# Decode step of a two-layer model: reordering the hand-over between layers, with fixed buffer slots and finer weight loads

## The chip, the cores and the metric

The kernel runs on one core of one Trainium2 chip. The metric is the device time of one execution in microseconds (us), lower is better. Before the change it is 533.6 us (median over 16 runs; 531.6 to 535.9 in the fast ones). One of those runs, the profiled one that the prediction was made from, took 668 us. It is of the slow state and is used in no comparison of times. Ratios below are the mean time of one kernel's fast runs over that of the other's fast runs of the same rounds, so they are not quite the ratio of the medians that are quoted.

## The reference

One token goes twice through attention and a gated MLP, with the same weights and the same caches both times. Cut to what matters:

```python
W = 4096                               # last W positions of a 32768-long cache
def attn(x):                           # 32 heads of 192; x is 1 x 640
    q = x @ wq                         # 640 -> 32*192
    s = einsum("hd,hkd->hk", q, k_cache[:, -W:]) * 192**-0.5
    return (softmax(s) @ v_cache[:, -W:]) @ wo
def mlp(x):  return (sigmoid(x @ w_gate) * (x @ w_up)) @ w_down      # 640 -> 1536 -> 640
for _ in range(2):
    x = x + attn(layernorm(x))
    x = x + mlp(layernorm(x))
```

There is one query per head, so nearly all the work is reading K and V: 16 head pairs, 7.3 MB each with their slices of `wq` and `wo`.

## The kernel before

All heavy data go through seven slots in SBUF (the on-chip memory), each of one unit of 3552 KB, plus a region `mreg` for MLP weights. Unit `a(p)` holds wq and K of head pair p, unit `b(p)` holds V and wo. At the end of layer 0 the seven slots are not freed: a(12) and a and b of pairs 13, 14 and 15 stay for layer 1, which therefore starts with these four pairs. V(12) is loaded again into `mreg` once the MLP is through with it.

```python
ORDER = [list(range(NPAIR)), [13, 14, 15, 12] + list(range(12))]
seq += stream(0, ORDER[0], [0])            # a0 a1 b0 a2 b1 ... a15 b14 b15 (two halves)
seq += [("wg",), ("u1",), ("u2",), ("d1",), ("d2",), ("va",), ("vb",), ("vc",)]
tail = stream(1, ORDER[1][4:], [0])        # layer 1: a0 a1 b0 a2 b1 ...
...
elif k == "u2":                            # second part of w_up, over the gate weights
    if "gate0" not in ev_done: return False
    pg.dma(... mreg(0, 5 * FW), wu_d[:, 7 * FW:] ...)
elif k in ("va", "vb", "vc"):              # V(12), over the MLP weights
    if "down0" not in ev_done: return False
```

The loads are issued from one queue, strictly in the order of `seq`; each waits until the region it overwrites has been read. TensorE, VectorE and ScalarE follow this loop:

```python
for i, p in enumerate(ORDER[l]):
    Q(p, y)              # 15 small matmuls: q of the pair
    QK(p, y)             # 24 matmuls 128x512, four column tiles side by side; then slot a(p) is free
    ...
    soft(p)              # maximum over the scores, exp
    ET(p, i % 2)         # transposes exp(scores)
    if prev is not None:
        PV(*prev)        # 32 matmuls 128x384 and the wo product of the pair before; then slot b is free
    prev = (p, i % 2)
```

In the MLP of layer 0 the gate is one block, and what overwrites it waits for all of it:

```python
proj(0, range(FC), g_of, 0, [...])         # gate: 12 blocks of 5 matmuls
if not last:
    mark("gate0")
```

## Time and profile before

| | slow profiled run | fast run |
|---|---|---|
| time, us | 668.0 | 533.6 (median) |
| bytes read from HBM | 219.18 MB | the same |
| rate while the DMA engines are full | 430 GB/s | not known before the prediction |
| one head pair in steady state | 19.26 us | not known before the prediction |

The page of the slow run: the busy time of the engines, then the span in 40 equal slices of 16.7 us. Each digit is the busy share in tenths, and GB/s is what the DMA engines moved.

```profile
span 666.2 us, 8191 instructions
PE 468.7 (70%) x3716; PEld 208.8 (31%) x3716; DVE 98.3 (15%) x372; ACT 88.6 (13%) x171; POOL 0.2 (0%) x4
...
DMA  8999999999999999360288784899899998995000
GB/s 357 436 432 429 426 430 434 429 430 429 429 437 426 426 432 371 148 290 1 110 293 325 311 363 184 363 409 399 363 371 370 370 367 387 416 369 226 0 1 3
```

For 250 us the DMA engines are full at about 430 GB/s. Then the stream has a hole between the layers, and never fills up again, because TensorE is slower than the stream in this run. The timeline of the same run shows one pair (start, duration, engine, line, operation; L350 is QK, L395 is PV):

```profile
104.89 4.92 PE L350 MATMUL scores<-big,qs 128*32 128x512 bf16 x24 [0.35 <-DVE qs L338]
...
116.12 4.90 PE L395 MATMUL bank<-big,et_sb 128*2 128x384 bf16 x32
...
124.17 4.91 PE L350 MATMUL scores<-big,qs 128*32 128x512 bf16 x24 [0.35 <-DVE qs L338]
```

From QK to QK it takes 19.28 us, but the pair's two units need only 2 x 3552 KB / 430 GB/s = 16.9 us. A run of 534 us is not possible at 19.3 us per pair (32 pairs would be 617 us), so in a fast run TensorE must be faster and the stream must bound. The stream alone needs 219.7 MB / 430 GB/s = 511 us. The question for the prediction was where the other 23 us of a fast run go.

### The profile page before, as it was taken

What the parts mean: (1) busy time and instruction counts of PE and PEld (TensorE: products, weight loads), DVE (VectorE), ACT (ScalarE), POOL (GpSimd) and SP (SyncE); (2) the same over time, 40 slices, a digit from 0 to 9 for tenths busy, and PEclk for the clock granted to TensorE, in tenths of its full rate; (3) what the DMA queues carried; (4) which work ended last, traced back from release to release, by engine and by line L of the source; (5) the groups of instructions that cost most, each with busy time, mean ns of one, the idle gap of its engine ahead of it and who ended that gap; (6) DMA issues with size and microseconds to landing.
All of it is one profiled execution on the core that took longest, in us unless ns stands there. A gap on an engine that the chain in (4) does not pass through costs nothing. (4 is left out here: it accounts for less than half of the span.)

```text
span 666.2 us, 8191 instructions
## 1 busy us (share of the span) xinstructions
PE 468.7 (70%) x3716; PEld 208.8 (31%) x3716; DVE 98.3 (15%) x372; ACT 88.6 (13%) x171; POOL 0.2 (0%) x4
## 2 busy tenths in 40 slices
PE   2676776777667677766765777667667766766776
PEld 1233232233223223332542323323223332233235
DVE  1111111110111111011012110111111011111101
ACT  0111111111111110111101011111110111111110
POOL 0000000000000000000000000000000000000000
DMA  8999999999999999360288784899899998995000
GB/s 357 436 432 429 426 430 434 429 430 429 429 437 426 426 432 371 148 290 1 110 293 325 311 363 184 363 409 399 363 371 370 370 367 387 416 369 226 0 1 3
DMA packets 10555, 219.71 MB, mean 330 GB/s; under 512 B 1304, under 2 KB 1304, under 8 KB 2200
## 3 DMA queue, kind: packets, MB, share of 16 engines
q1 hardware_dynamic: 10520, 219.19, 78.9%
q8 instruction: 29, 0.48, 0.3%
q14 instruction: 6, 0.05, 0.0%
HBM read 219.18 MB, written 0.00 MB: 329 GB/s over the span
## 5 line engine op out<-in xcount | busy, mean ns | idle before, releaser
L350 PE MATMUL scores<-big,qs 128*32 128x512 bf16 x768 | 157.7, 1046 | 11.0 <-DVE qs L338 10.5
L395 PE MATMUL bank<-big,et_sb 128*2 128x384 bf16 x1024 | 157.2, 855 | 0.0
L361 PE MATMUL bank<-diag,sc 128*128 128x128 f32 x64 | 32.2, 585 | 57.5 <-ACT diag L360 57.5
L395 PEld LDWEIGHTS bank<-big,et_sb 128*2 128x2 bf16 x1024 | 40.8, 164 | 74.2 <-issue 73.7
L359 DVE TENSOR_REDUCE sc<-scores 128x1 f32<-128x1024 f32 x32 | 39.2, 1225 | 151.6 <-PE scores L350 151.6
L350 PEld LDWEIGHTS scores<-big,qs 128*32 128x32 bf16 x768 | 34.8, 163 | 80.9 <-issue 67.6
L372 PE MATMUL bank<-cst,e_sb 128*128 128x8 bf16 x256 | 14.3, 179 | 61.5 <-ACT e_sb L366 61.5
L361 PEld LDWEIGHTS bank<-diag,sc 128*128 128x128 f32 x64 | 22.7, 395 | 110.0 <-ACT diag L360 110.0
L399 ACT CAST o_sb<-bank 128x384 bf16<-128x384 f32 x64 | 30.7, 479 | 196.5 <-PE bank L395 196.5
L360 ACT ACTIVATE diag<-cst,sc 128x128 f32<-128x128 bf16 x32 | 12.8, 401 | 267.2 <-DVE sc L359 267.2
L366 ACT ACTIVATE e_sb<-scores,sc 128x1024 bf16<-128x1024 f32 x32 | 38.5, 1204 | 52.2 <-DVE sc L364 52.2
L335 PE MATMUL bank<-sh,big 128*128 128x1 bf16 x480 | 29.5, 190 | 9.4 <-DMA big<-in_ua_dram 9.1
L379 PE MATMUL bank<-sc 128*128 128x2 f32 x64 | 24.8, 458 | 14.5 <-DVE sc L377 14.5
L372 PEld LDWEIGHTS bank<-cst,e_sb 128*128 128x128 bf16 x256 | 11.4, 119 | 70.9 <-ACT e_sb L366 70.9
L408 DVE TENSOR_SCALAR sh<-bank,sc 128x3 bf16<-128x3 f32 x32 | 7.2, 225 | 175.1 <-PE bank L405 175.1
L335 PEld LDWEIGHTS bank<-sh,big 128*128 128x128 bf16 x480 | 28.5, 153 | 9.5 <-DMA big<-in_ua_dram 9.2
L415 PE MATMUL bank<-sh,big 128*128 128x1 bf16 x480 | 23.8, 179 | 10.3 <-DVE sh L408 10.3
L379 PEld LDWEIGHTS bank<-sc 128*128 128x128 f32 x64 | 22.1, 385 | 17.5 <-DVE sc L377 17.5
L405 PEld LDWEIGHTS bank<-cst,o_sb 128*128 128x128 bf16 x192 | 7.6, 105 | 61.7 <-ACT o_sb L399 61.7
L415 PEld LDWEIGHTS bank<-sh,big 128*128 128x128 bf16 x480 | 21.1, 125 | 12.9 <-DVE sh L408 12.5
L405 PE MATMUL bank<-cst,o_sb 128*128 128x1 bf16 x192 | 10.2, 168 | 19.0 <-ACT o_sb L399 19.0
L362 DVE TENSOR_REDUCE sc<-bank 128x2 f32<-128x128 f32 x32 | 9.3, 292 | 49.1 <-PE bank L361 49.1
(55 smaller groups left out, 109.8 us busy)
## 6 DMA issues: line engine op xcount, KB each, us to landing
big<-in_ua_dram SPq DMA_DIRECT2D x28, 3552.0 KB, 20.8
big<-in_ub_dram SPq DMA_DIRECT2D x26, 3552.0 KB, 27.2
big<-in_ub_dram SPq DMA_DIRECT2D x2, 2016.0 KB, 7.4
big<-in_wg_dram SPq DMA_DIRECT2D x2, 1920.0 KB, 14.9
big<-in_ub_dram SPq DMA_DIRECT2D x2, 1536.0 KB, 10.7
big<-in_ub_dram SPq DMA_DIRECT2D x2, 1152.0 KB, 6.2
big<-in_wu_dram SPq DMA_DIRECT2D x1, 1920.0 KB, 14.4
big<-in_wu_dram SPq DMA_DIRECT2D x1, 1120.0 KB, 16.9
```

What stands on the lines that cost most here:

```text
L335: ins = t.matmul(qe[:, i:i + 1], lhsT=slot(sa, c * 2 * DH + c0, P), rhs=xq[:, c:c + 1], start=(c == 0), stop=(c == DC - 1))
L350: ins = t.matmul(bank[b][32 * j:32 * j + 32, :], lhsT=qs[:, y, k, :], rhs=slot(sa, WQE + k * W + (4 * b + j) * 512, 512), start=(k == 0), ...
L359: pg.op("dve", lambda v: v.reduce_max(out=mx, in_=scores[:], axis=AX.X), wr=[res("mx")], ex=[rb[0], rb[1]])
L360: pg.op("act", lambda a: a.mul(out=diag[:], in_=ident, mul=mx), rd=[res("cst"), res("mx")], wr=[res("diag")])
L361: pg.op("pe", lambda t: t.matmul(dmx[:, 0:P], lhsT=ones_f, rhs=diag[:], start=True, stop=True), rd=[res("diag"), res("ones")], ex=[rb[2]])
L366: pg.op("act", lambda a: a.activation(out=e_sb[:], in_=scores[:], func=ACT.Exp, bias=nbias, scale=srs_c, accum_out=rowsum), rd=[res("nbias ...
L372: ins = t.matmul(qe[:, 0:2 * NB].rearrange("p (r x) -> p r x", r=2)[:, :, 4 * b:4 * b + 4], lhsT=e_sb[:, b * P:(b + 1) * P], rhs=sel, star ...
L379: pg.op("pe", lambda t: t.matmul(dmx[:, P:P + 2], lhsT=ones_f, rhs=rs2, start=True, stop=True), rd=[res("rs2"), res("ones")], ex=[rb[2]])
L395: ins = t.matmul(o8[h][32 * j:32 * j + 2, 0:2 * DH].rearrange("p (a d) -> p a d", a=2), lhsT=et_sb[:, z, h * NB + 2 * u:h * NB + 2 * u + 2 ...
L399: pg.op("act", lambda a, h=h: a.copy(out=o8_sb[:, :, h * DH:(h + 1) * DH], in_=o8[h][:, 0:2 * DH].rearrange("p (a d) -> p a d", a=2)), wr= ...
L405: ins = t.matmul(oT3[:, c:c + 1], lhsT=o8_sb[:, sg, c:2 * DH:3], rhs=mask2[:, sg:sg + 1], start=(sg == 0), stop=(sg == 1))
L415: ins = t.matmul(yT[:, j:j + 1], lhsT=wo[:, c * D + j * P:c * D + (j + 1) * P], rhs=oTb[:, c:c + 1], start=False, stop=(c == 2), skip_grou ...
```

## The change

The intent is to keep the DMA queue full across the change of layer. The change has six parts: (1) the gate is cut into 5 + 7 blocks, and the loads over it wait for their own part; (2) the last V half of each layer is loaded and used in two quarters; (3) a(0) of layer 1 is loaded in two pieces, the first asked for after a third of QK(13); (4) the four kept pairs run in a new order, with QK(14) ahead of softmax 13 and its scores in the two PSUM banks of PV; (5) slots are assigned by a fixed table, with four slots in rotation in layer 0; (6) inside QK the loop over the three parts of the head dimension is the outer one. Cut to its core:

```diff
-    seq += [("wg",), ("u1",), ("u2",), ("d1",), ("d2",), ("va",), ("vb",), ("vc",)]
+    seq += [("wg", 0), ("wg", 1), ("u1",), ("u2",), ("d1",), ("d2",), ("va",), ("vb",), ("vc",)]
+    seq += [("a0", 0), ("a0", 1), ("wo12",)] + tail[1:]
+    A_SLOT = [{p: p % 2 ...}, ...]          # fixed slots; layer 0 rotates through four
...
-            mark("gate0")
+            mark("gate0", proj(0, range(GH), g_of, 0, [rm["a"]]))          # GH = 5
+            mark("gate1", proj(0, range(GH, FC), g_of, 0, [rm["b"]]))
...
-                for b in range(2):
-                    for k in range(3):
+                for k in ks:
+                    for b in range(2):
...
-        for i, p in enumerate(ORDER[l]):  ...    # one softmax at a time, also in layer 1
+            Q(13, 0); ...
+            mark("a13_0", QK(13, 0, ks=(0,)));  mark("a13_1", QK(13, 0, ks=(1, 2)))
+            Q(14, 1); ...; mark("Q12", Q(12, 0))
+            QK(14, 1, 1)                         # scores into the banks of PV
+            soft(0, scale_pm); expo(); Q(15, 1); ET(0)
+            soft(1); expo(1); QK(15, 1); PV(13, 0); ET(1)
+            soft(); expo(); PV(14, 1); QK(12, 0); ET(0)
+            soft(); expo(); PV(15, 0); Q(0, 0); ET(1); QK(0, 0); PV(12, 1); ...
```

No bytes are saved: both kernels read 219.18 MB.

More of the change, by code (lines that the diff above doesn't have):

```diff
@@ L1 @@
-from collections import deque
 from contextlib import ExitStack
@@ L155, in decode_kernel @@
     scores = ctx.enter_context(nc.psum_tensor("scores", [P, 1024], FP32))
-    bank = [scores[:, 0:512], scores[:, 512:1024]] + [ctx.enter_context(nc.psum_tensor(f"bank{i}", [P, 512], FP32)) for i in range(2, 8)]
+    bank = [scores[:, 0:512], scores[:, 512:1024]] + [ctx.enter_context(nc.psum_tensor(f"bank{i}", [P, 512], FP32)) for i in (2, 3)]
+    o8_ps = ctx.enter_context(nc.psum_tensor("o8", [P, 1024], FP32))
+    bank += [o8_ps[:, 0:512], o8_ps[:, 512:1024]] + [ctx.enter_context(nc.psum_tensor(f"bank{i}", [P, 512], FP32)) for i in (6, 7)]
     dmx, qe, o8, oT3, yT = bank[2], bank[3], bank[4:6], bank[6], bank[7]
@@ L167, in decode_kernel @@
     rslot = [res(f"slot{i}") for i in range(NSLOT)]
-    rm = {n: res("m_" + n) for n in ("a", "ax", "b", "c", "d")}
-    MOFF = {"a": (0, 3072), "b": (3072, 7680), "c": (7680, ME)}
+    rm = {n: res("m_" + n) for n in "abc"}
+    MOFF = {"a": (0, 5 * FW), "b": (5 * FW, 12 * FW), "c": (12 * FW, ME)}
     def slot(s, o, n):
@@ L180, in q_dma @@
         return lambda e: e.dma_start(out=o, in_=i)
-    RET = [("a", NPAIR - 4)] + [(k, p) for p in range(NPAIR - 3, NPAIR) for k in "ab"]
-    ORDER = [list(range(NPAIR)), [13, 14, 15, 12] + list(range(12))]
-    seq = []
-    def stream(l, ps, first):
-        out_ = [("a", l, p) for p in first]
-        q = deque(ps)
-        for p in ps[len(first):] if first else ps:
-            out_.append(("a", l, p))
-            out_.append(("b", l, q.popleft()))
-        last = list(q)
-        for p in last[:-1]:
-            out_.append(("b", l, p))
-        return out_ + [("b1", l, last[-1]), ("b0", l, last[-1])]
@@ L196, in decode_kernel @@
-    seq += stream(0, ORDER[0], [0])
-    seq += [("wg",), ("u1",), ("u2",), ("d1",), ("d2",), ("va",), ("vb",), ("vc",)]
-    tail = stream(1, ORDER[1][4:], [0])
-    seq += tail[:1] + [("wo12",)] + tail[1:]
+    A_SLOT = [{p: p % 2 for p in range(NPAIR)}, {p: 3 if p % 2 == 0 else 2 for p in range(NPAIR)}]
+    B_SLOT = [{p: 2 + p % 2 for p in range(NPAIR)}, {p: 5 if p % 2 else 0 for p in range(NPAIR)}]
+    A_SLOT[0].update({14: 4, 15: 6})
+    B_SLOT[0].update({14: 5, 15: 2})
+    A_SLOT[1].update({0: 1, 1: 4, **{p: A_SLOT[0][p] for p in (12, 13, 14, 15)}})
@@ new lines, in decode_kernel @@
+    B_SLOT[1].update({0: 6, **{p: B_SLOT[0][p] for p in (13, 14, 15)}})
+    KEPT = {(k, p) for p in (13, 14, 15) for k in "ab"} | {("a", 12)}
+    units = [("a", 0)] + [u for p in range(1, 12) for u in (("a", p), ("b", p - 1))] + [("b", 11), ("u", 0), ("d", 0)]
+    for i, (k, p) in enumerate(units):
+        s = (1, 0, 4, 6, 3, 5, 2)[(i if i == 0 else i + 1) % 7]
+        if k == "u":
+            U_SLOT = s
+        elif k == "d":
+            D_SLOT = s
+        else:
+            (A_SLOT if k == "a" else B_SLOT)[1][p] = s
@@ new lines, in decode_kernel, with stream @@
+    NHALF = NB * DH // 2
+    def stream(l, ps):
+        q = list(ps)
+        out_ = []
+        for i, p in enumerate(q):
+            out_.append(("a", l, p))
+            if i:
+                out_.append(("b", l, q[i - 1]))
+        return out_ + [("b1", l, q[-1]), ("b0", l, q[-1], 0), ("b0", l, q[-1], 1)]
+    seq = stream(0, range(NPAIR))
+    seq += [("wg", 0), ("wg", 1), ("u1",), ("u2",), ("d1",), ("d2",), ("va",), ("vb",), ("vc",)]
+    tail = stream(1, range(12))
+    assert tail[0] == ("a", 1, 0)
@@ L200, in decode_kernel, with wdp, take @@
+    seq += [("a0", 0), ("a0", 1), ("wo12",)] + tail[1:]
     seq += [("fg",), ("fu",), ("fd", 0), ("fd", 1), ("fd", 2)]
     seq_pos = [0]
-    free = deque(range(NSLOT))
-    where = {}
+    busy = set()
     ev_done = {}
-    fin = {}
-    wo12 = {}
-    halves = {}
-    pg_last = {}
-    def wdp(c0, c1, src=None):
-        return wd_d[:, c0 * D:c1 * D]
+    halves = {(0, NPAIR - 1), (1, 11)}
+    A0CUT = WQE + W
+    GH = 5
+    def wdp(c0, c1):
+        return wd_d[:, c0 * D:c1 * D]
+    def take(s):
+        if s in busy:
+            return False
+        busy.add(s)
+        return True
@@ L213, in try_load @@
     def try_load(it):
         k = it[0]
-        if k == "b0":
-            s = where[("b", it[2])]
-            pg.dma(q_dma(slot(s, 0, NB * DH), ub[it[2]][:, 0:NB * DH]), "bh", wr=[res("bh")], extra=list(pg_last["deps"].items()))
+        if k in ("a", "b"):
+            s = (A_SLOT if k == "a" else B_SLOT)[it[1]][it[2]]
+            if not take(s):
+                return False
+            pg.dma(q_dma(slot(s, 0, UNIT), (ua if k == "a" else ub)[it[2]]), f"s{s}", wr=[rslot[s]])
         elif k == "b1":
-            if not free:
-                return False
-            s = free.popleft()
-            where[("b", it[2])] = s
-            halves[(it[1], it[2])] = True
+            s = B_SLOT[it[1]][it[2]]
+            if not take(s):
+                return False
@@ L224, in try_load @@
             n = len(pg.ops["dma"])
             pg.dma(q_dma(slot(s, NB * DH, UNIT - NB * DH), ub[it[2]][:, NB * DH:]), f"s{s}", wr=[rslot[s]])
-            pg_last["deps"] = pg.ops["dma"][n]["deps"]
-        elif k in "ab":
-            if not free:
-                return False
-            s = free.popleft()
-            where[(k, it[2])] = s
-            pg.dma(q_dma(slot(s, 0, UNIT), (ua if k == "a" else ub)[it[2]]), f"s{s}", wr=[rslot[s]])
+            ev_done["b1"] = list(pg.ops["dma"][n]["deps"].items())
+        elif k == "b0":
+            s = B_SLOT[it[1]][it[2]]
+            o = it[3] * NHALF
+            pg.dma(q_dma(slot(s, o, NHALF), ub[it[2]][:, o:o + NHALF]), f"bh{it[3]}", wr=[res(f"bh{it[3]}")], extra=ev_done["b1"])
+        elif k == "a0":
+            if f"a13_{it[1]}" not in ev_done:
+                return False
+            s = A_SLOT[1][0]
+            o0, o1 = ((0, A0CUT), (A0CUT, UNIT))[it[1]]
+            pg.dma(q_dma(slot(s, o0, o1 - o0), ua[0][:, o0:o1]), f"a0{it[1]}", wr=[res(f"a0{it[1]}")] + ([rslot[s]] if it[1] else []),
+                   extra=[ev_done[f"a13_{it[1]}"]])
@@ L233, in try_load @@
         elif k == "wg":
-            pg.dma(q_dma(mreg(0, 12 * FW), wg_d), "wg", wr=[rm["a"], rm["ax"], rm["b"]])
+            f0, f1 = ((0, GH), (GH, FC))[it[1]]
+            pg.dma(q_dma(mreg(f0 * FW, (f1 - f0) * FW), wg_d[:, f0 * FW:f1 * FW]), f"wg{it[1]}", wr=[[rm["a"]], [rm["b"]]][it[1]])
         elif k == "u1":
-            pg.dma(q_dma(mreg(12 * FW, 7 * FW), wu_d[:, 0:7 * FW]), "u1", wr=[rm["c"], rm["d"]])
+            pg.dma(q_dma(mreg(12 * FW, 7 * FW), wu_d[:, 0:7 * FW]), "u1", wr=[rm["c"]])
@@ L239, in try_load @@
                 return False
-            pg.dma(q_dma(mreg(0, 5 * FW), wu_d[:, 7 * FW:]), "u2", wr=[rm["a"], rm["ax"]])
+            pg.dma(q_dma(mreg(0, 5 * FW), wu_d[:, 7 * FW:]), "u2", wr=[rm["a"]])
         elif k == "d1":
-            pg.dma(q_dma(mreg(5 * FW, 7 * FW), wdp(0, 7)), "d1", wr=[rm["b"]])
+            if "gate1" not in ev_done:
+                return False
+            pg.dma(q_dma(mreg(5 * FW, 7 * FW), wdp(0, 7)), "d1", wr=[rm["b"]], extra=[ev_done["gate0"]])
         elif k == "d2":
@@ L250, in try_load @@
             o0, o1 = MOFF[k[1]]
-            pg.dma(q_dma(mreg(o0, o1 - o0), ub[12][:, o0:o1]), k, wr={"a": [rm["a"]], "b": [rm["ax"], rm["b"]], "c": [rm["c"], rm["d"]]}[k[1]])
+            pg.dma(q_dma(mreg(o0, o1 - o0), ub[12][:, o0:o1]), k, wr=[rm[k[1]]])
         elif k == "wo12":
@@ L254, in try_load @@
                 return False
-            s = where[("a", 12)]
-            wo12["ap"] = slot(s, 0, WOE)
-            pg.dma(q_dma(wo12["ap"], ub[12][:, VE:UNIT]), "wo12", wr=[res("wo12")], extra=[ev_done["Q12"]])
+            pg.dma(q_dma(slot(A_SLOT[1][12], 0, WOE), ub[12][:, VE:UNIT]), "wo12", wr=[res("wo12")], extra=[ev_done["Q12"]])
         elif k == "fg":
-            pg.dma(q_dma(mreg(0, 12 * FW), wg_d), "wg", wr=[rm["a"], rm["ax"], rm["b"], rm["c"], rm["d"]])
+            pg.dma(q_dma(mreg(0, 12 * FW), wg_d), "fg", wr=[rm["a"], rm["b"], rm["c"]])
         elif k == "fu":
-            if not free:
+            if not take(U_SLOT):
                 return False
-            fin["u"] = s = free.popleft()
-            pg.dma(q_dma(slot(s, 0, 12 * FW), wu_d), f"s{s}", wr=[rslot[s]])
-        else:
-            if it[1] == 0:
-                if not free:
-                    return False
-                fin["d"] = free.popleft()
-            s = fin["d"]
+            pg.dma(q_dma(slot(U_SLOT, 0, 12 * FW), wu_d), f"s{U_SLOT}", wr=[rslot[U_SLOT]])
+        else:
+            if it[1] == 0 and not take(D_SLOT):
+                return False
             c0, c1 = WFIN[it[1]]
-            pg.dma(q_dma(slot(s, c0 * D, (c1 - c0) * D), wdp(c0, c1)), f"wf{it[1]}", wr=[rslot[s]] if it[1] == 0 else [])
+            pg.dma(q_dma(slot(D_SLOT, c0 * D, (c1 - c0) * D), wdp(c0, c1)), f"wf{it[1]}", wr=[rslot[D_SLOT]] if it[1] == 0 else [])
         return True
@@ L283, in release @@
     def release(s):
-        free.append(s)
+        busy.discard(s)
         prefetch()
@@ L327, in attention @@
         pg.op("dve", lambda v: v.memset(yT[:, 0:DC], 0.0), ex=[rb[7]])
+        S = [(scores, bank[0], bank[1], rb[0], rb[1]), (o8_ps, bank[4], bank[5], rb[4], rb[5])]
         def Q(p, y):
-            sa = where[("a", p)]
+            sa = A_SLOT[l][p]
             def f(t):
@@ L336, in f, with QK, soft @@
                 return ins
-            ev = pg.op("pe", f, rd=[res("xq"), rslot[sa]], ex=[rb[3]])
+            ev = pg.op("pe", f, rd=[res("xq"), rslot[sa]] + ([res("a00")] if l == 1 and p == 0 else []), ex=[rb[3]])
             pg.op("dve", lambda v: v.tensor_tensor(out=qs[:, y], in0=qe[:, 0:3].unsqueeze(2).to_broadcast([P, 3, 32]), in1=mask3, op=ALU.mult),
                   rd=[res("cst")], wr=[res(f"qs{y}")], ex=[rb[3]])
-            if l == 1 and p == 12:
-                mark("Q12", ev)
-        def QK(p, y):
-            sa = where[("a", p)]
+            return ev
+        def QK(p, y, x=0, ks=(0, 1, 2)):
+            sa = A_SLOT[l][p]
+            sc_x = S[x]
             def f(t):
-                for b in range(2):
-                    for k in range(3):
+                for k in ks:
+                    for b in range(2):
                         for j in range(4):
-                            ins = t.matmul(bank[b][32 * j:32 * j + 32, :], lhsT=qs[:, y, k, :], rhs=slot(sa, WQE + k * W + (4 * b + j) * 512, 512),
+                            ins = t.matmul(sc_x[1 + b][32 * j:32 * j + 32, :], lhsT=qs[:, y, k, :], rhs=slot(sa, WQE + k * W + (4 * b + j) * 512, 512),
                                            start=(k == 0), stop=(k == 2), tile_position=(0, 32 * j))
                 return ins
-            pg.op("pe", f, rd=[res(f"qs{y}"), rslot[sa]], ex=[rb[0], rb[1]])
-            if l == 1 or ("a", p) not in RET:
-                if not (l == 1 and p == 12):
-                    release(sa)
-        def soft(p):
-            pg.op("dve", lambda v: v.reduce_max(out=mx, in_=scores[:], axis=AX.X), wr=[res("mx")], ex=[rb[0], rb[1]])
+            ev = pg.op("pe", f, rd=[res(f"qs{y}"), rslot[sa]] + ([res("a00"), res("a01")] if l == 1 and p == 0 else []), ex=sc_x[3:5])
+            if ks[-1] == 2 and not (l == 0 and ("a", p) in KEPT) and not (l == 1 and p in (12, 13)):
+                release(sa)
+            return ev
+        def soft(x=0, hook=None):
+            sc_x = S[x]
+            pg.op("dve", lambda v: v.reduce_max(out=mx, in_=sc_x[0][:], axis=AX.X), wr=[res("mx")], ex=sc_x[3:5])
+            if hook is not None:
+                hook()
             pg.op("act", lambda a: a.mul(out=diag[:], in_=ident, mul=mx), rd=[res("cst"), res("mx")], wr=[res("diag")])
@@ L365, in soft, with expo, ET @@
                   rd=[res("nb2"), res("pm_s")], wr=[res("nbj"), res("nbias")], multi=True)
-            pg.op("act", lambda a: a.activation(out=e_sb[:], in_=scores[:], func=ACT.Exp, bias=nbias, scale=srs_c, accum_out=rowsum),
-                  rd=[res("nbias"), res("srs")], wr=[res("e"), res("rowsum")], ex=[rb[0], rb[1]], multi=True)
-        def ET(p, z):
+        def expo(x=0):
+            sc_x = S[x]
+            pg.op("act", lambda a: a.activation(out=e_sb[:], in_=sc_x[0][:], func=ACT.Exp, bias=nbias, scale=srs_c, accum_out=rowsum),
+                  rd=[res("nbias"), res("srs")], wr=[res("e"), res("rowsum")], ex=sc_x[3:5], multi=True)
+        def ET(z):
             def f(t):
@@ L385, in PV, with f @@
             inm = l == 1 and p == 12
-            sv = where.get(("b", p))
-            half = halves.pop((l, p), False)
+            sv = None if inm else B_SLOT[l][p]
+            half = (l, p) in halves
             for h in (1, 0) if half else (0, 1):
-                rV = list(rm.values()) if inm else [rslot[sv]] if not (half and h == 0) else [rslot[sv], res("bh")]
                 vt = (mreg(h * NB * DH, NB * DH) if inm else slot(sv, h * NB * DH, NB * DH)).rearrange("p (t d) -> p t d", t=NB)
-                def f(t, h=h, vt=vt):
-                    for u in range(NB // 2):
-                        j = u % 4
-                        ins = t.matmul(o8[h][32 * j:32 * j + 2, 0:2 * DH].rearrange("p (a d) -> p a d", a=2), lhsT=et_sb[:, z, h * NB + 2 * u:h * NB + 2 * u + 2],
-                                       rhs=vt[:, 2 * u:2 * u + 2, :], start=(u < 4), stop=(u >= NB // 2 - 4), tile_position=(0, 32 * j))
-                    return ins
-                pg.op("pe", f, rd=[res(f"et{z}")] + rV, ex=[rb[4 + h]])
+                for part in (0, 1) if half and h == 0 else (None,):
+                    us = range(NB // 2) if part is None else range(part * NB // 4, (part + 1) * NB // 4)
+                    def f(t, h=h, vt=vt, us=us):
+                        for u in us:
+                            j = u % 4
+                            ins = t.matmul(o8[h][32 * j:32 * j + 2, 0:2 * DH].rearrange("p (a d) -> p a d", a=2), lhsT=et_sb[:, z, h * NB + 2 * u:h * NB + 2 * u + 2],
+                                           rhs=vt[:, 2 * u:2 * u + 2, :], start=(u < 4), stop=(u >= NB // 2 - 4), tile_position=(0, 32 * j))
+                        return ins
+                    rV = list(rm.values()) if inm else [rslot[sv]] + ([] if part is None else [res(f"bh{part}")])
+                    pg.op("pe", f, rd=[res(f"et{z}")] + rV, ex=[rb[4 + h]])
                 pg.op("act", lambda a, h=h: a.copy(out=o8_sb[:, :, h * DH:(h + 1) * DH], in_=o8[h][:, 0:2 * DH].rearrange("p (a d) -> p a d", a=2)),
@@ L409, in PV @@
                   rd=[res(f"Rn{z}0"), res(f"Rn{z}1")], wr=[res("oTb")], ex=[rb[6]])
-            wo = wo12["ap"] if inm else slot(sv, VE, WOE)
+            wo = slot(A_SLOT[1][12], 0, WOE) if inm else slot(sv, VE, WOE)
             def im(t):
@@ L417, in im @@
                 return ins
-            sa = where[("a", p)]
+            sa = A_SLOT[1][12]
             pg.op("pe", im, rd=[res("oTb")] + ([res("wo12"), rslot[sa]] if inm else [rslot[sv]]), ex=[rb[7]])
@@ L421, in PV @@
                 release(sa)
-            elif l == 1 or ("b", p) not in RET:
+            elif not (l == 0 and ("b", p) in KEPT):
                 release(sv)
-        prev = None
-        early = {}
-        for i, p in enumerate(ORDER[l]):
-            if p in early:
-                y = early[p]
-            else:
-                y = 0
-                Q(p, y)
-            QK(p, y)
-            if i == 0:
-                ln_sq(xi)
-                ln_rstd(K2_ATT, eps_a, srs_c, res("srs"))
-                pg.op("dve", lambda v: v.tensor_scalar(out=pm_s, in0=pm, scalar1=srs_c, scalar2=None, op0=ALU.mult),
-                      rd=[res("cst"), res("srs")], wr=[res("pm_s")])
-                if l == 1:
-                    early[12] = 1
-                    Q(12, 1)
-            soft(p)
-            ET(p, i % 2)
-            if prev is not None:
-                PV(*prev)
-            prev = (p, i % 2)
@@ L447, in attention, with scale_pm, scored @@
-        PV(*prev)
+        def scale_pm():
+            pg.op("dve", lambda v: v.tensor_scalar(out=pm_s, in0=pm, scalar1=srs_c, scalar2=None, op0=ALU.mult),
+                  rd=[res("cst"), res("srs")], wr=[res("pm_s")])
+        def scored(p):
+            Q(p, 0)
+            QK(p, 0)
+            soft()
+            expo()
+            ET(p % 2)
+        if l == 0:
+            Q(0, 0)
+            ln_sq(xi)
+            QK(0, 0)
+            ln_rstd(K2_ATT, eps_a, srs_c, res("srs"))
+            soft(0, scale_pm)
+            expo()
+            ET(0)
+            first, n = 0, NPAIR
+        else:
+            Q(13, 0)
+            ln_sq(xi)
+            mark("a13_0", QK(13, 0, ks=(0,)))
+            mark("a13_1", QK(13, 0, ks=(1, 2)))
+            Q(14, 1)
+            ln_rstd(K2_ATT, eps_a, srs_c, res("srs"))
+            mark("Q12", Q(12, 0))
+            QK(14, 1, 1)
+            soft(0, scale_pm)
+            expo()
+            Q(15, 1)
+            ET(0)
+            soft(1)
+            expo(1)
+            QK(15, 1)
+            PV(13, 0)
+            ET(1)
+            soft()
+            expo()
+            PV(14, 1)
+            QK(12, 0)
+            ET(0)
+            soft()
+            expo()
+            PV(15, 0)
+            Q(0, 0)
+            ET(1)
+            QK(0, 0)
+            PV(12, 1)
+            soft()
+            expo()
+            ET(0)
+            first, n = 0, 12
@@ L448, in attention @@
+        for p in range(first, n - 1):
+            scored(p + 1)
+            PV(p, p % 2)
+        PV(n - 1, (n - 1) % 2)
         return residual(xi)
@@ L481, in mlp @@
         g_of = lambda fb: mreg(fb * FW, FW)
-        proj(0, range(FC), g_of, 0, [rm["a"], rm["ax"], rm["b"]] + ([rm["c"], rm["d"]] if last else []))
-        if not last:
-            mark("gate0")
+        if last:
+            proj(0, range(FC), g_of, 0, [rm["a"], rm["b"], rm["c"]])
+        else:
+            mark("gate0", proj(0, range(GH), g_of, 0, [rm["a"]]))
+            mark("gate1", proj(0, range(GH, FC), g_of, 0, [rm["b"]]))
         ln_rstd(K2_MLP, eps_m, rstd_c, res("rstd"))
@@ L487, in mlp @@
         if last:
-            u_of = lambda fb: slot(fin["u"], fb * FW, FW)
-            ru = [[rslot[fin["u"]]]] * 2
+            u_of = lambda fb: slot(U_SLOT, fb * FW, FW)
+            ru = [[rslot[U_SLOT]]] * 2
         else:
             u_of = lambda fb: mreg(12 * FW + fb * FW, FW) if fb < 7 else mreg((fb - 7) * FW, FW)
-            ru = [[rm["c"], rm["d"]], [rm["a"], rm["ax"]]]
+            ru = [[rm["c"]], [rm["a"]]]
         ubank = (1, 6)
@@ L535, in finish @@
                     i = nc.tensor.matmul(yrow[32 * g:32 * g + 1, 0:RW], lhsT=hT[:, c:c + 1],
-                                         rhs=slot(fin["d"], c * D + g * RW, RW),
+                                         rhs=slot(D_SLOT, c * D + g * RW, RW),
                                          start=False, stop=(c == FC - 1), skip_group_check=True, tile_position=(0, 32 * g))
```

## The prediction

> **What bounds it now.** The kernel moves 219.2 MB (the page's HBM line). Where the DMA engines are full (DMA share 1.00 in the windows from 50 to 250 us) they move 429 to 432 GB/s[...]. So the stream alone needs about 509 us. The three fast runs take 532 to 536 us. First bytes move at about 2.5 us, some 5 us of work follow the last byte, and launch adds 2: about 15 us of a fast run are unexplained, and I take them for a DMA queue that runs dry in the middle.
>
> The profiled run is not a fast run (668 us). In it TensorE sets the pace: a head pair takes 19.26 us (timeline), of which QK 5.0 and PV 5.0, while its data take 16.9. Each round of four column-tiled 128x512 matmuls takes 0.84 us. [...] this trace shows 205 ns per matmul. A fast run must be below 16.9 us a pair, so there the DMA stream bounds, and TensorE matters only where the next load waits for a buffer.
>
> **Where the queue runs dry (timeline, SP waits).** After the last V of layer 0, all seven slots hold pairs kept for layer 1. The second half of `up` waits for the whole gate projection (60 matmuls, 3.0 us); `down` and V follow in latency-bound steps; then a(0) waits for QK of pair 13, a(1) for QK14 (21.5 us after `down` ended), b(0) for PV13 (34.7), because softmax and PV stand between. Counting with QK and PV at about 3 us instead of 5 (an estimate from the gap between 668 and 534), I get about 3 us idle before `up`, 1 around V, and 1.5 to 4 at each of four slot waits: 13 to 14 us. [...]
>
> **What the change does.** No bytes and nearly no work are removed. Gate is split 5 + 7, so the second half of `up` is issued 35 matmuls (1.8 us) earlier and follows the queue without a gap. The last V loads are halved (-0.5 us). a(0) comes in two parts, the first after a third of QK13. Q14, Q12 and QK14 come before softmax 13, with scores in the PV banks, so a(1) is issued some 6 us earlier, b(0) (now after QK15) and b(1) 10 or more. Static slots leave layer 0 with four buffers; a(p+2) is still asked for about 20 us before its turn, so this costs nothing. The new matmul order inside QK: worth nothing.
>
> On the critical path, then: about 11 us of the idle queue. Fast runs: 535 -> 523 us, range 517 to 531. No gap at all would give 518. Faster by over 2%: 0.52, within 2%: 0.46, slower: 0.02.
>
> **What would show it.** In the profile: the DMA slices between 250 and 420 us fill up; the second `up` load is issued before gate ends; a(1) is issued right after QK14, with no softmax before it; from QK13 to QK(0) about 57 us instead of 70.6, and `down` ends 3 to 4 us earlier. If the profile is again in the slow TensorE state, its span falls by about 19 us, to some 647 us; pairs stay at 19.3 us.
>
> **What would make it wrong.** Fast TensorE being so fast that the queue hardly runs dry (then 530, within 2%); the 15 us lying elsewhere, such as a lower DMA rate without the profiler; four buffers in layer 0 being too few; small DMAs costing more latency than their earlier start wins.

Two of the terms as measured: launch is the 668.0 us of the slow run less its span of 666.2 us; in the "latency-bound steps" TensorE waited 2.40 us for the second part of `up` and 2.63 us for `down` to land (331.73 and 335.74 us of that run).

## The result, and the profile after

The changed kernel takes 527.95 us (median of 11 runs, 526.3 to 529.8). The ratio to before is 0.9897 with a 95% interval of 0.9878 to 0.9915: 1.0% faster, which counts as the same at a limit of 2%. A second set of runs gave 0.9910 (0.9893 to 0.9927).

This time the profile fell in the fast state. The kernel before was profiled again (run `before_again`), and that one was fast too. All comparisons of traces below use these two. The page of the kernel before, in slices of 13.3 us:

```profile
span 530.5 us, 8191 instructions
...
PEclk9997655555556566655555557556656656566555
DMA  8999999999999999999997999999999999999994
GB/s 341 431 430 436 421 436 432 426 434 426 428 434 433 428 430 424 434 433 428 432 415 308 364 397 370 438 421 437 423 432 432 425 433 428 428 434 426 426 420 193
```

The page of the kernel after, in slices of 13.2 us:

```profile
span 526.7 us, 8201 instructions
...
PEclk9996555555566655656565556665666666666555
DMA  8999999999999999999998999999999999999994
GB/s 344 429 433 426 434 426 435 425 433 429 431 429 430 433 429 432 424 436 426 433 411 328 352 439 432 429 431 426 435 426 429 431 427 431 432 427 429 425 424 204
```

In both the stream is full from the second slice to the second last, but for a dip between about 265 and 330 us. Before, the dip covers five slices (415, 308, 364, 397, 370); after, only three (411, 328, 352). The change filled the later part of the dip and left the earlier part.

The same in windows, for the kernel before. The columns are the stretch and its length, the busy time of the engines, the granted TensorE clock, the DMA share and GB/s. (The clock of 1.00 in the first line, and the first digits of PEclk above, are taken for missing records and not for readings: in the kernel after, QK takes 2.75 us there too, at 13.87 and at 23.33 us, as it does at 296.24 us, where the clock reads 0.50.)

```profile
0.00:20.00 20.00, 5.13 (x45) 2.76 (x45) 3.42 (x16) 2.15 (x4) 0.20 (x4) 1.00 0.90 368
20.00:276.00 256.00, 130.21 (x1587) 63.11 (x1586) 44.03 (x157) 41.45 (x78) 0.00 (x0) 0.59 1.00 430
276.00:304.00 28.00, 14.57 (x281) 10.49 (x281) 4.52 (x26) 2.18 (x8) 0.00 (x0) 0.50 0.89 338
304.00:330.00 26.00, 14.03 (x185) 7.53 (x189) 6.32 (x25) 5.64 (x10) 0.00 (x0) 0.63 0.96 386
330.00:510.00 180.00, 109.29 (x1377) 52.50 (x1366) 37.15 (x130) 35.44 (x67) 0.00 (x0) 0.57 1.00 429
510.00:530.50 20.50, 11.08 (x257) 7.96 (x253) 2.85 (x19) 1.69 (x5) 0.00 (x0) 0.50 0.65 272
```

And for the kernel after:

```profile
0.00:20.00 20.00, 5.22 (x45) 2.78 (x45) 3.89 (x19) 2.33 (x5) 0.20 (x4) 1.00 0.91 371
20.00:276.00 256.00, 129.05 (x1590) 62.30 (x1594) 43.59 (x154) 41.42 (x78) 0.00 (x0) 0.59 1.00 429
276.00:304.00 28.00, 17.89 (x334) 12.01 (x327) 4.63 (x26) 2.08 (x7) 0.00 (x0) 0.50 0.91 346
304.00:330.00 26.00, 16.27 (x195) 7.94 (x192) 6.55 (x27) 6.50 (x12) 0.00 (x0) 0.59 1.02 435
330.00:510.00 180.00, 104.93 (x1345) 51.12 (x1345) 36.63 (x129) 35.37 (x67) 0.00 (x0) 0.60 1.00 429
510.00:526.70 16.70, 8.05 (x217) 7.10 (x217) 2.85 (x19) 0.73 (x3) 0.00 (x0) 0.50 0.61 251
```

A stretch of T us at R GB/s loses T x (1 - R/430) us of the full stream. That gives a balance of the span. It adds up by construction, so the sum proves nothing; what tells is where the loss lies. The stretch from 20 to 276 us is left out: 1 GB/s there is 0.6 us, so the sums are good to about half a us.

| us lost against 430 GB/s | before (fast) | after |
|---|---|---|
| start, 0 to 20 us | 2.9 | 2.7 |
| MLP of layer 0, 276 to 304 us | 6.0 | 5.5 |
| waits for slots of the kept pairs, 304 to 330 us | 2.7 | none |
| 330 to 510 us | 0.4 | 0.4 |
| end, from 510 us | 7.5 | 7.0 |
| 219.71 MB at 430 GB/s | 511 | 511 |
| sum | 530.5 | 526.6 |

The two spans differ by 3.9 us, the times of the two kernels (0.9897 of 533 us) by about 5.5: this pair of profiles locates some 4 us of the gain and not all of it.

The one item that vanishes is the waits for slots. The MLP's loss is not a sharp number: a second profile of the same kernel (`after_again`) has 367 GB/s in that window, a loss of 4.1 us instead of 5.5. So a difference of about 1.5 us in that row can come from run to run.

One part of that row is sharp, though: the 6 us around the gate and the second load of `up`. First the kernel before, then the kernel after, then two single microseconds of the kernel after:

```profile
280.00:286.00 6.00, 4.28 (x114) 3.94 (x112) 1.34 (x11) 0.73 (x3) 0.00 (x0) 0.50 0.53 176
...
280.00:286.00 6.00, 4.16 (x107) 3.81 (x104) 1.11 (x10) 0.73 (x3) 0.00 (x0) 0.50 0.76 270
...
280.00:281.00 1.00, 0.74 (x10) 0.61 (x7) 0.17 (x2) 0.00 (x0) 0.00 (x0) 0.50 0.77 323
281.00:282.00 1.00, 0.65 (x24) 0.64 (x24) 0.54 (x6) 0.00 (x0) 0.00 (x0) 0.50 0.54 224
```

The loss there falls from 3.5 to 2.2 us. The profiles of all the fast runs below agree: 3.4 to 3.6 us in the four kernels with an unsplit gate (`before_again`, `slots_only`, `order_only`, `gate_whole`), 1.7 to 2.5 us in the nine with a split one. Part of it is lost again from 286 to 293 us: 0.1 to 0.2 us with the unsplit gate, 0.5 to 1.4 with the split one. The last two lines show why cutting the gate can't close this gap: the stream is already down to 323 and 224 GB/s around the start of the gate (281.39 us), and a load over the gate weights can't go out before the gate has used some of them.

The timeline shows why the slot waits vanish. In the kernel before (SPq is the queue that issues loads; `in_ua` are units a, `in_ub` units b; L478 is gate and up, L350 QK, L395 PV):

```profile
281.75 1.76 PE L478 MATMUL scores<-sh,big 128*128 128x1 bf16 x60 [0.48 <-DMA big<-in_wg_dram]
...
283.53 0.33 SPq L180 DMA_DIRECT2D big<-in_wu_dram  x1
...
296.97 2.75 PE L350 MATMUL scores<-big,qs 128*32 128x512 bf16 x24 [0.44 <-DVE sc L304]
...
299.76 0.33 SPq L180 DMA_DIRECT2D big<-in_ua_dram  x1
...
307.75 2.75 PE L350 MATMUL scores<-big,qs 128*32 128x512 bf16 x24 [0.35 <-DVE qs L338]
...
310.54 0.33 SPq L180 DMA_DIRECT2D big<-in_ua_dram  x1
...
316.38 2.73 PE L395 MATMUL bank<-big,et_sb 128*2 128x384 bf16 x32
...
320.90 0.33 SPq L180 DMA_DIRECT2D big<-in_ub_dram  x1
321.59 1.48 PE L350 MATMUL scores<-big,qs 128*32 128x512 bf16 x24 [0.35 <-DVE qs L338]
```

In the kernel after (L542 is gate and up, L372 QK, L424 PV):

```profile
281.39 1.94 PE L542 MATMUL scores<-sh,big 128*128 128x1 bf16 x60 [0.35 <-DVE sc L324]
...
282.23 0.33 SPq L181 DMA_DIRECT2D big<-in_wu_dram  x1
...
296.24 2.75 PE L372 MATMUL scores<-big,qs 128*32 128x512 bf16 x24 [0.44 <-DVE sc L324]
...
297.32 2.04 SPq L181 DMA_DIRECT2D big<-in_ua_dram  x2
...
300.33 2.75 PE L372 MATMUL o<-big,qs 128*32 128x512 bf16 x24
...
303.12 0.33 SPq L181 DMA_DIRECT2D big<-in_ua_dram  x1
...
312.92 0.33 SPq L181 DMA_DIRECT2D big<-in_ub_dram  x1
```

Before, QK(14) starts 10.8 us after QK(13), because softmax 13 stands between them; a(1) is asked for at 310.54. After, it starts 4.1 us after QK(13), and a(1) is asked for at 303.12. V(0) comes 8 us earlier (312.92 instead of 320.90). The second load of `w_up` is issued at 282.23, while the gate still runs, instead of at 283.53 after its end; that is 1.3 us earlier, but QK(13) starts only 0.7 us earlier.

### The profile page after: what moved, and what is told of

The parts are those of the page before. It is cut to its first block, busy times and chain, and to the rows that moved or that the text cites. A ratio compares the mean times of both kernels' runs of the same rounds, so it can differ in the third digit from the quotient of the medians.

```text
span 526.7 us, 8201 instructions
## 1 busy us (share of the span) xinstructions
PE 281.4 (53%) x3716; PEld 143.3 (27%) x3716; DVE 98.2 (19%) x372; ACT 88.4 (17%) x171; POOL 0.2 (0%) x4
## 2 busy tenths in 40 slices
DMA packets 11131, 219.71 MB, mean 417 GB/s; under 512 B 1368, under 2 KB 1368, under 8 KB 2904
## 3 DMA queue, kind: packets, MB, share of 16 engines
HBM read 219.18 MB, written 0.00 MB: 416 GB/s over the span
## 5 line engine op out<-in xcount | busy, mean ns | idle before, releaser
L372 PE MATMUL scores<-big,qs 128*32 128x512 bf16 x744 | 84.0, 621 | 9.9 <-DVE qs L360 9.4
L424 PE MATMUL o<-big,et_sb 128*2 128x384 bf16 x1024 | 87.2, 516 | 2.4 <-DMA big<-in_ub_dram 2.4
L429 ACT CAST o_sb<-o 128x384 bf16<-128x384 f32 x64 | 30.7, 479 | 117.5 <-PE o L424 117.5
L357 PE MATMUL bank<-sh,big 128*128 128x1 bf16 x480 | 17.7, 166 | 60.2 <-DMA big<-in_ua_dram 59.9
L386 PE MATMUL bank<-diag,sc 128*128 128x128 f32 x64 | 20.2, 408 | 54.6 <-ACT diag L385 54.6
L424 PEld LDWEIGHTS o<-big,et_sb 128*2 128x2 bf16 x1024 | 29.0, 114 | 40.3 <-issue 34.2
L372 PEld LDWEIGHTS scores<-big,qs 128*32 128x32 bf16 x744 | 24.3, 134 | 44.5 <-issue 32.4
L386 PEld LDWEIGHTS bank<-diag,sc 128*128 128x128 f32 x64 | 12.6, 246 | 79.1 <-ACT diag L385 79.1
L357 PEld LDWEIGHTS bank<-sh,big 128*128 128x128 bf16 x480 | 15.8, 105 | 62.6 <-DMA big<-in_ua_dram 61.4
L360 DVE TENSOR_TENSOR qs<-bank,cst 128x96 bf16<-128x96 f32 x32 | 8.2, 258 | 93.7 <-PE bank L357 93.6
L445 PE MATMUL bank<-sh,big 128*128 128x1 bf16 x480 | 17.8, 166 | 10.3 <-DVE sh L438 10.3
L445 PEld LDWEIGHTS bank<-sh,big 128*128 128x128 bf16 x480 | 15.2, 104 | 12.9 <-DVE sh L438 12.5
```

What stands on the lines that cost most here:

```text
L357: ins = t.matmul(qe[:, i:i + 1], lhsT=slot(sa, c * 2 * DH + c0, P), rhs=xq[:, c:c + 1], start=(c == 0), stop=(c == DC - 1))
L372: ins = t.matmul(sc_x[1 + b][32 * j:32 * j + 32, :], lhsT=qs[:, y, k, :], rhs=slot(sa, WQE + k * W + (4 * b + j) * 512, 512), start=(k == ...
L386: pg.op("pe", lambda t: t.matmul(dmx[:, 0:P], lhsT=ones_f, rhs=diag[:], start=True, stop=True), rd=[res("diag"), res("ones")], ex=[rb[2]])
L424: ins = t.matmul(o8[h][32 * j:32 * j + 2, 0:2 * DH].rearrange("p (a d) -> p a d", a=2), lhsT=et_sb[:, z, h * NB + 2 * u:h * NB + 2 * u + 2 ...
L429: pg.op("act", lambda a, h=h: a.copy(out=o8_sb[:, :, h * DH:(h + 1) * DH], in_=o8[h][:, 0:2 * DH].rearrange("p (a d) -> p a d", a=2)), wr= ...
L445: ins = t.matmul(yT[:, j:j + 1], lhsT=wo[:, c * D + j * P:c * D + (j + 1) * P], rhs=oTb[:, c:c + 1], start=False, stop=(c == 2), skip_grou ...
```

## The experiments

All runs gave correct results. Each was timed in five rounds against the kernel before on the same chip; the chip differs between groups of runs (4, 7 and 12), so ratios of different groups that differ by 0.1 or 0.2% say little. For each, the ratio to before is given with its 95% interval.

### The kernel before again

No edit.

> The kernel before, unchanged: the noise floor, and a second chance of a profile in the fast state. Time: 1.00 of before within 0.2%. If the profile is fast: a round of four column-tiled 128x512 matmuls takes about 0.43 us as in the profile after (not 0.84), and the DMA queue loses about 11 to 12 us against 430 GB/s between the last load of layer 0 and the end of the kept pairs, against 5.8 us after. Theory S (slot waits): most of the extra 5.6 us lies after the MLP, at the waits for the slots of QK14 and PV13. Rival G (gate): most of it lies before the MLP's end, at the second up load and the V loads.

Measured: 532.49 us, ratio 0.9988 (0.9969 to 1.0006). So the method resolves about 0.2%, or 1 us. The profile is the fast one used above: QK takes 2.75 us instead of 4.9, and the losses are 6.0 us around the MLP and 2.7 us at the slot waits. Between this profile and the one of the kernel after, these two rows shrink by 3.2 us, of which 2.7 are slot waits, as theory S (the expectation above names it) says. The losses are smaller than the 11 to 12 us that I expected.

### The old order of the kept pairs, in the new kernel

```diff
-            Q(14, 1); ...; QK(14, 1, 1); soft(0, scale_pm); expo(); Q(15, 1); ET(0); soft(1); ...
+            soft(0, scale_pm); expo(); ET(0)
+            Q(14, 0); QK(14, 0); soft(); expo(); ET(1); PV(13, 0)
+            Q(15, 0); QK(15, 0); soft(); expo(); ET(0); PV(14, 1); ...
-        s = (1, 0, 4, 6, 3, 5, 2)[...]      # slots in the order in which they come free
+        s = (1, 0, 4, 3, 6, 5, 2)[...]
```

> The kernel after, with the four kept pairs of layer 1 in the old order, one softmax at a time (QK14 only after the exponentials of 13 are transposed), slots remapped to the order in which that frees them. Theory S: loses most of the gain, +3.5 to +5.5 us on after (531.5 to 533.5 us), with idle DMA at the loads of K1 and V0 of layer 1. Rival G: under +1 us (below 529).

Measured: 531.83 us, ratio 0.9979 (0.9951 to 1.0008). Against 0.9897 and 0.9910 for the whole change, 0.7 to 0.8% is lost, about 4 us: most of the gain. Most of the loss at the slot waits is back. Its windows:

```profile
276.00:304.00 28.00, 14.05 (x273) 10.29 (x273) 4.66 (x27) 3.25 (x9) 0.00 (x0) 0.50 0.93 356
304.00:330.00 26.00, 15.34 (x197) 7.79 (x197) 6.18 (x23) 4.99 (x12) 0.00 (x0) 0.63 0.97 393
```

393 GB/s in the second window is a loss of 2.2 us. By the times, rival G (under 529 us) is out.

### The gate unsplit

```diff
-            mark("gate0", proj(0, range(GH), g_of, 0, [rm["a"]]))
-            mark("gate1", proj(0, range(GH, FC), g_of, 0, [rm["b"]]))
+            ev_g = proj(0, range(FC), g_of, 0, [rm["a"], rm["b"]])
+            ev_done["gate0"] = ev_g
+            mark("gate1", ev_g)
```

Both loads over the gate weights stay, but each now waits for the whole gate.

> The kernel after, with both of the loads that reuse the gate weights waiting for all 12 gate blocks instead of the first 5. Theory S: +0.5 to +1.5 us (35 matmuls, about 1.1 us in the fast state, fully exposed because the queue is empty there). Rival G: +3 us or more.

Measured: 529.16 us, ratio 0.9920 (0.9903 to 0.9938). That is 0.5 to 1.2 us worse than the change, the size that theory S gave; but the intervals overlap, so from the times it is only likely that the split is worth something, about 1 us. The profile is clearer: from 280 to 286 us it loses 3.5 us (180 GB/s), as the kernel before does, against 2.2 with the split.

### The last V half in one piece

```diff
-    out_ + [("b1", l, q[-1]), ("b0", l, q[-1], 0), ("b0", l, q[-1], 1)]
+    out_ + [("b1", l, q[-1]), ("b0", l, q[-1], 0)]
```

> The kernel after, with the last V half of each layer loaded and used whole instead of in two quarters. Both theories: the chain from that landing to the gate starts one quarter of PV later, about 0.7 us, at the end of layer 0; at the end of layer 1 it is hidden behind the last weight loads. So +0.5 to +0.9 us.

Measured: 528.07 us, ratio 0.9899 (0.9880 to 0.9918), equal to the change. The profile has a span of 527.4 us against 526.7, but the times don't confirm it. A gain of the V quarters is not shown.

### The kernel after again

No edit.

> The kernel after, unchanged, as the yardstick of this call: 0.990 of before (527 to 529 us).

Measured: 527.86 us, ratio 0.9910 (0.9893 to 0.9927), span 525.8 us.

### K(0) of layer 1 asked for in one go

```diff
-            mark("a13_0", QK(13, 0, ks=(0,)))
-            mark("a13_1", QK(13, 0, ks=(1, 2)))
+            ev_q = QK(13, 0)
+            ev_done["a13_0"] = ev_q
+            mark("a13_1", ev_q)
```

The edit leaves the two loads of K(0) as they are; both now wait for the whole of QK(13). So it tests the earlier request, not one load against two.

> The kernel after, with K(0) of layer 1 loaded as one piece after the whole of QK13 instead of in two pieces. The first piece is now asked for about 1.8 us earlier, while the last V12 loads should still be in flight. Theory (the V loads cover it): +0 to +0.5 us. Rival (the queue is already empty there, as the profile after suggests between 294 and 299 us): +1 to +2 us.

Measured: 527.96 us, ratio 0.9905 (0.9889 to 0.9921), equal to the change. K(0) was asked for at 298.32 instead of 297.32 us, and this cost nothing that can be measured. The rival's 2 us are out; its 1 us is at the edge of what the intervals exclude.

### The fixed slots and the QK loop alone

The new kernel with the last four edits together (old order, gate, V and K(0) whole), so only parts (5) and (6) and the two loads each of the gate weights and of K(0) remain.

> The kernel after with the serial order of the kept pairs, gate, V and K(0) all in the old form: what is left of the change is the fixed slots (four buffers in layer 0), the order of the matmuls inside QK, and gate weights landing in two loads. Theory (these are worth nothing): equal to before within 0.3%. Rival (four buffers cost time that the rest of the change must first win back): slower than before by 2 us or more.

Measured: 532.49 us, ratio 0.9993 (0.9973 to 1.0013): equal to before. Four buffers in layer 0 cost nothing, and these parts win nothing.

### The new order alone

`slots_only` with the new order of the kept pairs and nothing else.

> slots_only plus the new order of the kept pairs and nothing else: one part of the change done alone. If the parts add up (serial_l1 lost about 3.7 us of the gain, gate_whole about 1), it is at 0.9925 to 0.994 of before (529 to 530 us), and its DMA queue loses nothing after 304 us while the loss around the MLP stays at 6.2 us as in before_again. If early QK14 only pays together with the split loads, it stays above 0.996.

Measured: 529.45 us, ratio 0.9923 (0.9901 to 0.9946). So adding the order to a kernel that equals before wins 0.7%, as much as taking it out of the whole change loses. Windows of `slots_only`, then of `order_only`:

```profile
276.00:304.00 28.00, 14.54 (x281) 10.50 (x281) 4.67 (x27) 2.28 (x8) 0.00 (x0) 0.50 0.89 337
304.00:330.00 26.00, 14.25 (x189) 7.59 (x193) 6.19 (x23) 5.78 (x11) 0.00 (x0) 0.63 0.97 392
```

```profile
276.00:304.00 28.00, 17.30 (x320) 11.73 (x321) 4.47 (x25) 2.08 (x7) 0.00 (x0) 0.50 0.89 338
304.00:330.00 26.00, 16.26 (x205) 8.14 (x204) 6.72 (x27) 6.49 (x12) 0.00 (x0) 0.66 1.02 438
```

The first window is the same (337 and 338 GB/s); only the second fills, from 392 to 438. The order acts where it was meant to, and nowhere else. It is the one part whose worth the times show clearly.

### A warm TensorE, first try

```diff
+            if hot: warm(12)      # 12 spare 256-column matmuls, before Q of pairs 14 and 15 of layer 0
             Q(p, 0)
             QK(p, 0)
+            if hot: warm(7)       # and again in the two waits of softmax
```

> The kernel after, with 52 spare 256-column matmuls into unused PSUM columns during TensorE's waits in the last two pairs of layer 0[...]. Outputs unchanged. Theory R (the 5.8 us that the DMA queue still loses around the MLP is a chain of landing, TensorE, issue): the granted clock between 275 and 300 us rises from about 0.5 to near 1.0 and 1 to 2 us are won (526 to 527 us). Rival L (those 5.8 us are only landing and issue latency, or small transfers at a lower rate): no change beyond 0.3 us though the clock rises.

Measured: 528.33 us, ratio 0.9917 (0.9901 to 0.9934). The clock was 0.71 from 270 to 280 us (0.50 in the kernel after), but 0.50 in the MLP, from 276 to 304 us, so the experiment did not do what it was to do, and tells nothing about R or L.

### Finer cuts in the MLP

```diff
-            mark("gate0", proj(0, range(GH), ...)); mark("gate1", proj(0, range(GH, FC), ...))
+            mark("gate00", proj(0, range(2), ...)); mark("gate01", proj(0, range(2, GH), ...)); mark("gate1", ...)
-    ("u2",), ("d1",), ("d2",), ("va",), ("vb",), ("vc",)
+    ("u2", 0), ("u2", 1), ("d1", 0), ("d1", 1), ("d2",), ("va",), ("vb",), ("vd",), ("vc",)
```

> The kernel after with the MLP of layer 0 cut finer: gate 2+3+7 blocks, the second up load 2+3, the first down load 4+3, and the V12 load over it 4+3, each asked for as soon as its own part of the region is free. Theory R (the rest of the loss is a chain of landing, TensorE, issue): the second up load starts 0.4 us earlier and V12 over the down weights about 1 us earlier, so 0.5 to 1.5 us are won (0.988 of before). Rival L (small transfers and landings cost as much as the earlier start wins): within 0.2% of after (0.9895 to 0.992).

Measured: 528.77 us, ratio 0.9908 (0.9887 to 0.9930): no gain. The last line below shows that K(0) was not asked for earlier (297.72 against 297.32 us):

```profile
282.29 0.80 SPq L182 DMA_DIRECT2D big<-in_wu_dram  x2
...
297.72 2.04 SPq L182 DMA_DIRECT2D big<-in_ua_dram  x2
```

### A warm TensorE, second try

Spare matmuls in every wait of the chain from the last V quarter of layer 0 to QK(13), for example:

```diff
+            warm(5)               # after the first part of up, while the second part is still landing
             proj(ubank[1], range(7, FC), u_of, 1, ru[1], 7)
...
+            warm((10, 3)[i])      # before each part of down
```

> The kernel after with spare matmuls not only before the MLP of layer 0 but in every wait of the chain through it (warm_pe cooled down before the MLP and told nothing). Outputs unchanged. If the granted clock between 275 and 300 us rises clearly above 0.5: theory R expects the MLP chain to shorten by 1 to 2 us and the time to fall to 526 to 527 us (0.988); rival L expects no change. If the clock stays at 0.5, it tells nothing, and the spare matmuls may cost up to 1 us.

Measured: 528.27 us, ratio 0.9899 (0.9878 to 0.9920). The granted clock in the MLP was 0.50 again, with TensorE busy for 9.25 of 10 us. One window of this run:

```profile
280.00:290.00 10.00, 9.25 (x145) 6.59 (x144) 1.56 (x12) 0.73 (x3) 0.00 (x0) 0.50 0.84 295
```

By its own terms this run tells nothing about R or L. It does show that 79 spare matmuls in the waits cost no time.

### wo behind the last V quarters

```diff
-            pg.dma(q_dma(slot(s, NB * DH, UNIT - NB * DH), ub[it[2]][:, NB * DH:]), ...)   # V half and wo
+            pg.dma(q_dma(slot(s, NB * DH, NB * DH), ub[it[2]][:, NB * DH:VE]), ...)        # V half
+        elif k == "bw":                                                                  # wo, after the quarters
+            pg.dma(q_dma(slot(s, VE, WOE), ub[it[2]][:, VE:UNIT]), "bw", ...)
```

> The kernel after, with the 480 KB of the output projection that ride on the first half of each layer's last V load moved behind the V quarters as a load of their own. Same bytes; at the end of layer 0 the last V quarter lands 1.1 us earlier (480 KB at 430 GB/s), and 1.1 us more of loads stand between it and the empty queue. Theory R (the rest of the loss is the chain from that landing to the second up load): the chain to K(0) moves up by about 1 us and 0.7 to 1.2 us are won (0.9875 to 0.9885 of before, 526.7 to 527.3 us). Rival L (cost of landings and small transfers): no gain, 0.9895 to 0.992.

Measured: 527.67 us, ratio 0.9904 (0.9887 to 0.9920): no gain. The second load of `w_up` was issued 0.9 us earlier than in the kernel after (281.33 against 282.23), but K(0) at the same time (297.20 against 297.32):

```profile
281.33 0.33 SPq L181 DMA_DIRECT2D big<-in_wu_dram  x1
...
297.20 2.03 SPq L181 DMA_DIRECT2D big<-in_ua_dram  x2
```

So theory R in the form that I gave it falls: the chain that the last V landing starts is not what sets the time of K(0). No version was found that beats the kernel after.

## Why the prediction was right or wrong

The class (within 2%) and the range (517 to 531 us) held. The centre, 523 us, was 5 us too low, and faster by over 2% had been given slightly better odds than what happened. The mechanism was right; the sizes in the sum were not. That the number still fell in the range owes much to the range's width of 14 us: 528 us lies nearer to the 530 that the prediction names for the case that the queue hardly runs dry than to its centre.

- **The stream bounds the fast run: right.** Between 20 and 276 us the fast runs move 429 to 430 GB/s, and 511 us of the 526.7 us are the stream.
- **QK and PV at about 3 us in a fast run: right** (2.75 and 2.73 us). The four column tiles do run side by side there: 24 matmuls of 512 columns in 2.75 us are 0.115 us each, while 10 of the spare untiled matmuls of 256 columns in `warm_chain` took 2.29 us (at 287.40 us), which is 0.46 us per 512 columns, at the same granted clock of 0.50.
- **"1.5 to 4 at each of four slot waits": too large.** With 1 us around V and 3 before `up`, it was part of an idle sum of 13 to 14 us; the slot waits after 304 us measure 2.7 us. (The first of the four, for K(0), lies before that; the whole stretch from 293 to 304 us loses 2.1 us in both kernels.) The term that was mis-sized is the duration of a kept pair in the old order. I took only the savings on QK and PV off the slow 19.26 us, which leaves about 15.2 (the prediction does not print this step). In a fast run the rest of TensorE's work is faster too (the 15 matmuls of Q take 0.56 instead of 0.95 us), and V(0) and V(1) were asked for at 320.90 and 333.14 us, 12.2 us apart. So the slots came free sooner, and the old order lost less than I thought. That this accounts for the whole difference is argued, not shown.
- **The second `up` load "follows the queue without a gap": wrong.** It was issued before the gate ended, as predicted, but the window around the MLP still loses 5.5 us (4.1 in the second profile), against 6.0 before; of that, 2.2 us (2.1) lie between 280 and 286 us, where the stream runs down before the gate starts. This is the second term that was mis-sized: the prediction counted on 11 of 13 to 14 us of the idle queue, and the profiles show 3.2 of 8.7 recovered (4.6 with the second profile).
- **"About 15 us of a fast run are unexplained, and I take them for a DMA queue that runs dry in the middle": too large.** 8.7 us lie in the middle. The start and end lose 2.9 and 7.5 us; I had put 2.5 and 5.
- **a(1) "some 6 us earlier", b(0) and b(1) "10 or more": roughly right.** It was 7.4 us for a(1), 8.0 us for b(0) and 7.5 us for b(1) (325.59 instead of 333.14).
- **"From QK13 to QK(0) about 57 us instead of 70.6", "`down` ends 3 to 4 us earlier": too large.** From QK(13) to QK(0) it was 49.9 us before (296.97 to 346.89) and 42.0 after (296.24 to 338.28), 7.9 us less instead of 13.6. `down` ends 0.7 us earlier (294.12 instead of 294.86).
- **Fixed slots and the QK loop worth nothing: right** (`slots_only` is 0.9993 of before). **The V quarters at 0.5 us: not shown.**
- **The slow state** (a span of some 647 us): not tested, because no later profile fell into it. QK took 4.92 us in the slow run, against 2.75 us at a granted clock of 0.50 and 1.48 us at one of 1.00 (296.24 and 378.46 us of the kernel after); the page of the slow run has no PEclk row, so its clock is not known. What puts a run into it is open.

What remains open is the rest of the loss of 4 to 5.5 us around the MLP, beyond the run-down before the gate. Asking for the second `up` load earlier (`wo_last`), cutting the loads finer (`fine_split`) and asking for K(0) later (`k_whole`) all leave the time where it is. Whether many small transfers cost something there (rival L) is not decided either. The kernel before waits for its first part of `up` until 284.43 us, the kernel after until 284.94. I suspect that this landing, and the loads for the rest of the MLP behind it, set the time of K(0); that is argued from the timelines and not shown.

## What to carry to other kernels

In a kernel bound by its DMA stream, look for the places where a load waits for a buffer, and turn the compute order so that buffers come free early: here one reordered softmax was worth 0.7%, and three finer splits of loads together about 1 us, which the intervals hardly separate from nothing. Size such a gain as lost stream (length of the stretch times one minus rate over full rate) from a profile of the same state as the timed runs; a profile from another state gives the mechanism, but not the sizes. Before counting on closing a gap, look when the stream begins to run down: here that was 280 us, 1.4 us before the gate started, and splitting the gate took the loss of the next 6 us from 3.5 to 2.2 us and not to zero.
